# Later DRAM transposing and a later sum beside accumulating loads, in a pooled-attention and MoE kernel

## The chip, the cores and the metric

One core of one Trainium2 chip. The metric is the device time of one execution in microseconds (us); lower is better. Before: 985.83 us, the median of 3 runs (984.55 to 986.24).

## The reference

Four batches of attention, whose keys and values are 4x4 mean-pooled `kv` times a small weight, followed by an MLP with a quick gelu on all 49152 tokens.

```python
kv_pool = kv.reshape(B, H // r, r, W // r, r, C).mean(axis=(2, 4))       # B=4, r=4, C=128
kv_flat = kv_pool.reshape(B, -1, C) @ w_sr
k = v = kv_flat                                                          # 768 keys per batch
a = softmax(1 / sqrt(C) * (q @ k.transpose(0, 2, 1)))                    # 12288 queries per batch
x = (a @ v).reshape(B * S, D)
h = x @ w_in                                                             # d_ff = 2048
out = (h * (1.0 / (1.0 + np.exp(-1.702 * h)))) @ w_out
```

## The kernel before

The program has two rounds: attention on two batches (48 groups of 512 tokens), then the MLP ("MoE") on the same 48 groups. `x`, the attention's result, stays in SBUF, the on-chip memory. TensorE fills three banks of PSUM (the memory that its results go to), ScalarE applies exp or gelu to 128x1536 values at a time, and TensorE multiplies the result by the next weight. The MoE needs `x` transposed. The first 72 of a round's 192 blocks of 128 tokens are transposed on TensorE (`turn`); the other 120 go out to DRAM (the buffer `x_bf`) and come back through the transposing DMA, in six parts of 20 blocks. Both DMAs, and the output stores, are issued by SyncE, in program order:

```python
def put_away(n, m):
    o = LATER + m * PART                                   # LATER, PART = 72, 20
    lo = n * XS * SG + o * T
    nc.sync.dma_start(out=x_bf[lo:lo + PART * T, :].rearrange("(k p) c -> p k c", p=T),
                      in_=x[:, o * T:(o + PART) * T].rearrange("p (k c) -> p k c", k=PART))

def bring_back(n, m):
    ...
    nc.sync.dma_start_transpose(out=x[:, o * T:(o + PART) * T].unsqueeze(1), in_=x_bf[lo:lo + PART * T, :])
```

In the first round's MoE the keys of batches 2 and 3 are made for the second round. Eight steps of two loads each add up `kv` in the DMA (two halves, `i2`; each load but the first of a half accumulates, and waits for the one before it). A `gate`, a tiny memset on VectorE that GpSimd waits for, keeps them one step to a group. Then VectorE adds the two halves, and TensorE transposes the sum:

```python
def add_kv(b, n):
    i, w = divmod(n, r)
    ...
    for i2 in range(2):
        nc.gpsimd.dma_start(out=kv_sums[b][:, i2], in_=kv_p[b, i, w, :, i2],
                            **({"accum_op": ADD} if n else {}))

def sum_kv(b, a):
    t = kv_sums[b][:, :, 4 * a:4 * a + 4, :]
    pooled[b, a] = kvtmp.tile([Hp, 4, C], BF, name="pooled")
    nc.vector.tensor_tensor(pooled[b, a], t[:, 0], t[:, 1], ADD)

def use_kv(b, a):
    sum_kv(b, a)
    extras.extend([(transpose_pooled, b, a), (make_k, b, a), (make_v, b, a)])   # TensorE, placed soon after

def background_moe(g):                                     # called as group g's first matmuls are placed
    n, g = divmod(g, 4 * XS)                               # n: round; 4 * XS = 48
    m, odd = divmod(g - 3, 2)
    if 0 <= m < (4 * XS * G // T - LATER) // PART:         # six parts
        (bring_back if odd else put_away)(n, m)
    g += n * 4 * XS
    for b, lo in ((2, 2), (3, 20)):
        if lo <= g < lo + 8:
            gate()
            add_kv(b, g - lo)
        if g in (lo + 9, lo + 13):
            use_kv(b, (g - lo - 9) // 4)
```

A finished group's output is transposed by VectorE into one of three `o_sb` buffers and stored by SyncE in four DMAs. Cuts are marked with dots.

The softmax here doesn't subtract the row's maximum and nothing guards it: scores larger than these inputs give would overflow.

Of the kernel before, what the change touches and what calls it, by code (L numbers as in the profile page):

```python
# [20 lines left out]
def kernel(  # L21
# [134 lines left out]
    def add_kv(b, n):  # L156
        i, w = divmod(n, r)
        if n == 0:
            kv_sums[b] = kvsum.tile([Hp, 2, Wp, C], F32, name="kvs")
# [8 lines that stand above are left out]
# [209 lines left out]
    def gate():  # L377

        nc.vector.memset(gate_tile, 0.0)  # L379
        nc.gpsimd.memset(gate_tile, 0.0)  # L380
# [27 lines left out]
    def background_moe(g):  # L408

        n, g = divmod(g, 4 * XS)  # L410
        m, odd = divmod(g - 3, 2)
        if 0 <= m < (4 * XS * G // T - LATER) // PART:
            (bring_back if odd else put_away)(n, m)
        g += n * 4 * XS
        for b, lo in ((2, 2), (3, 20)):
            if lo <= g < lo + 8:
                gate()
                add_kv(b, g - lo)
            if g in (lo + 9, lo + 13):
                use_kv(b, (g - lo - 9) // 4)  # L420

    def use_kv(b, a):
        sum_kv(b, a)
        extras.extend([(transpose_pooled, b, a), (make_k, b, a), (make_v, b, a)])
# [36 lines left out]
    for n in range(R):  # L461
        part = chunks[n * NA // R:(n + 1) * NA // R]
        while part:
            m = sizes.pop(0) if sizes else K
# [17 lines left out]
    def prepare(p):  # L482

        nonlocal now
        for f, *args in first.get(p, ()):
            if f in COST:
                now = max(now, free[next_acc()])
            f(*args)
            if f in COST:
                now += COST[f][0]  # L490
                free[last_acc] = now + COST[f][1]
        kind, part = seq[p]
        for i, _ in part:
            if (kind, i) not in begun:
                begun.add((kind, i))
                (background if kind == "a" else background_moe)(i)
# [119 lines left out]
```

## Time and profile before

| | kernel before |
|---|---|
| median of 3 runs, us | 985.83 |
| profiled execution: time, span, us | 987.93, 986.1 |
| ScalarE busy, us | 956.0 |
| ScalarE idle before gelu (line L435), us | 8.5 |
| ScalarE idle before exp (L321), us | 11.7 |

In the page's groups the number after the bar is busy time, then the mean of one instruction in ns, then the engine's idle time just before these instructions and what ended it. ScalarE is the bound where its idle time is nearly nil. Times in timelines are microseconds from the span's start. The rows are shown in the prediction below.

### The profile page before, as it was taken

Reading aid. Unit: us, or ns where it says so; the run is one execution under the profiler, and the core shown is the slowest. Engines: PE = TensorE matmul, PEld = TensorE weight load, DVE = VectorE, ACT = ScalarE, POOL = GpSimd, SP = SyncE. Lnnn points to the kernel's source line nnn. Section 1 sums busy time; section 2 is a strip of 40 time slices with the busy share of each in tenths; the row PEclk is TensorE's granted clock in tenths of the full one; section 3 lists DMA queues with packets and bytes.
Section 4 is the critical chain, followed back from the end, with each engine's and each line's share of the span. In section 5 each row is a group of like instructions: output and inputs, shape, how many; then the busy total and the mean of one; then the engine's idle time right before and its main releaser. Section 6 shows DMA issues by size and latency. Waiting matters only on the chain.

```text
span 986.1 us, 15763 instructions
## 1 busy us (share of the span) xinstructions
PE 963.7 (98%) x6431; PEld 513.1 (52%) x6431; DVE 207.7 (21%) x506; ACT 956.0 (97%) x713; POOL 65.4 (7%) x113
## 2 busy tenths in 40 slices
PE   7899999997999999999999999999999999999997
PEld 3567777543444444444447777754444444444443
DVE  4444333201110111101114433320111010101010
ACT  4999999996999999999999999999999999999997
POOL 3100101320002310000000000000000000000000
PEclk9999999998999999999999999999999999999999
DMA  9897764999628972222276432025772222222222
GB/s 181 160 200 147 108 118 85 121 164 178 115 35 121 157 97 43 35 41 43 41 105 113 86 77 59 2 38 110 136 141 40 44 43 33 38 39 34 41 32 43
DMA packets 335688, 84.99 MB, mean 86 GB/s; under 512 B 309568, under 2 KB 333248, under 8 KB 335296
## 3 DMA queue, kind: packets, MB, share of 16 engines
q1 hardware_dynamic: 305456, 51.34, 31.1%
q0 software_dynamic: 29104, 32.51, 22.0%
q8 instruction: 50, 0.82, 0.3%
q10 hardware_dynamic: 1056, 0.13, 0.1%
q14 instruction: 22, 0.18, 0.1%
HBM read 52.49 MB, written 43.52 MB: 97 GB/s over the span
## 4 chain that ended last, share of the span: by engine, by line
PE 62%; ACT 26%; DMA 5%; issue 4%; DVE 1%; POOL 1%; POOLq 0%; DVEq 0%; ACTq 0%
ACT ag L435 24%; PE banks L440 19%; PE banks L433 18%; PE banks L330 12%; PE banks L319 12%; DMA kvs<-in_kv_dram 4%; ACT ag L321 2%; POOL kvs L161 1%; PE banks L356 1%; DMA x<-in_q_dram 1%; DVE qT L224 1%; PE banks L218 0%; PE banks L129 0%; PE banks L265 0%; DVE xt L346 0%
## 5 line engine op out<-in xcount | busy, mean ns | idle before, releaser
L435 ACT ACTIVATE ag<-banks 128x1536 bf16<-128x1536 f32 x512 | 690.1, 1531 | 8.5 <-PE banks L433 8.5
L433 PE MATMUL banks<-x,w_in_sb 128*128 128x512 bf16 x1536 | 415.9, 379 | 0.4 <-ACT ag L435 0.3
L440 PE MATMUL banks<-ag,w_out_sb 128*128 128x512 bf16 x1536 | 411.5, 380 | 0.5 <-ACT ag L435 0.5
L321 ACT ACTIVATE ag<-banks 128x1536 bf16<-128x1536 f32 (+2 forms) x196 | 260.2, 1451 | 11.7 <-PE banks L319 11.3
L440 PEld LDWEIGHTS <-w_out_sb 128*128 128x128 bf16 x1536 | 149.9, 98 | 180.6 <-issue 1.4
L433 PEld LDWEIGHTS <-w_in_sb 128*128 128x128 bf16 x1536 | 148.4, 98 | 180.4 <-issue 24.1
L447 DVE STREAM_TRANSPOSE o_sb<-banks 128x512 f32<-128x512 f32 x96 | 68.8, 716 | 554.2 <-PE banks L440 554.2
L330 PEld LDWEIGHTS <-ag 128*128 128x128 bf16 x2304 | 150.2, 97 | 48.1 <-issue 1.5
L330 PE MATMUL banks<-v,ag 128*128 128x129 bf16 x2304 | 168.7, 220 | 0.7 <-DVE v L153 0.7
L319 PE MATMUL banks<-qT,kT 128*128 128x512 bf16 x576 | 155.8, 378 | 5.7 <-ACT ag L321 4.1
L319 PEld LDWEIGHTS <-kT 128*128 128x128 bf16 x576 | 48.9, 97 | 33.5 <-issue 4.2
L338 DVE RECIPROCAL rec<-banks 128x3 f32<-128x3 f32 x128 | 23.0, 180 | 132.3 <-PE banks L330 132.3
L346 DVE TENSOR_TENSOR x<-banks,rec 128x384 bf16<-128x384 f32 x80 | 44.6, 558 | 2.8
L161 POOL DMA_DIRECT2D kvs<-in_kv_dram x32 | 40.2, 1307 | 36.9 <-DMA kvs<-in_kv_dram 34.0
L380 POOL MEMSET gate_tile<- 1x8 f32 x38 | 4.5, 119 | 458.0 <-DVE gate_tile L379 458.0
L346 DVE TENSOR_TENSOR xt<-banks,rec 128x384 bf16<-128x384 f32 x48 | 26.8, 558 | 1.7
L358 DVE COPY x<-banks 128x768 bf16<-128x768 bf16 x24 | 13.4, 558 | 24.5 <-PE banks L356 24.5
L356 PE MATMUL banks<-ident,xt 128*128 128x128 bf16 x144 | 11.9, 218 | 0.0
L224 DVE COPY qT<-banks 128x512 bf16<-128x512 bf16 x15 | 9.8, 687 | 5.0 <-PE banks L218 4.9
L195 POOL DMA_DIRECT2D q_bf<-in_q_dram x20 | 9.9, 496 | 5.3 <-DMA x<-in_q_dram 1.9
L356 PEld LDWEIGHTS <-xt 128*128 128x128 bf16 x144 | 9.3, 97 | 1.4
L218 PE MATMUL banks<-ident,x 128*128 128x128 bf16 x64 | 6.0, 224 | 2.6 <-DVE qT L224 1.9
(56 smaller groups left out, 87.7 us busy)
## 6 DMA issues: line engine op xcount, KB each, us to landing
out_dram<-o_sb SPq DMA_DIRECT2D x382, 64.0 KB, 2.0
kvs<-in_kv_dram POOLq DMA_DIRECT2D x32, 384.0 KB, 6.4
q_bf<-in_q_dram POOLq DMA_DIRECT2D x20, 512.0 KB, 6.5
x_bf<-x SPq DMA_DIRECT2D x12, 640.0 KB, 4.7
x<-in_kv_dram POOLq DMA_DIRECT2D x12, 512.0 KB, 12.4
x<-in_q_dram POOLq DMA_DIRECT2D x3, 512.0 KB, 20.3
w_in_sb<-in_moe_w_in_dram POOLq DMA_DIRECT2D x1, 512.0 KB, 5.1
w_out_sb<-in_moe_w_out_dram POOLq DMA_DIRECT2D x1, 512.0 KB, 7.6
```

The costliest lines, as they stand in the source:

```text
L161: nc.gpsimd.dma_start(out=kv_sums[b][:, i2], in_=kv_p[b, i, w, :, i2], **({"accum_op": ADD} if n else {}))
L224: nc.vector.tensor_copy(dst, src)
L319: nc.tensor.matmul(ps[:, k, :], kTs[i // GB][:, jc * 128:(jc + 1) * 128], rhs, start=True, stop=True)
L321: nc.scalar.activation(place([("a",) + c for c in chunks]), ps, AF.Exp, scale=scale)
L330: nc.tensor.matmul(av_of[u][:, k * (C + 1):(k + 1) * (C + 1)], weights(("a", i, jc))[:, o:o + T], vs[i // GB][:, jc, 0:C + 1], start=(jc = ...
L338: nc.vector.reciprocal(rec, ps[:, :, C])
L346: nc.vector.tensor_tensor(to, ps[:, :, 0:C], rec.unsqueeze(2).broadcast_to([128, TS, C]), MUL)
L356: nc.tensor.transpose(ps[:, k, :], xt[:, k, :], ident)
L433: nc.tensor.matmul(ps[:, k, :], w_in_sb[:, fc * 128:(fc + 1) * 128], x[:, g % (4 * XS) * G:(g % (4 * XS) + 1) * G], start=True, stop=True)
L435: nc.scalar.activation(place([("m",) + c for c in chunks]), ps, AF.Gelu_apprx_sigmoid)
L440: nc.tensor.matmul(o_of[g], w_out_sb[:, fc, :], weights(("m", g, fc)), start=(fc == 0), stop=(fc == FCH - 1))
L447: nc.vector.transpose(o_sb, o_of.pop(g))
```

## The change

Its intent: keep the DRAM transposing away from the accumulating loads. Batch 2's loads run at groups 2 to 9, so the transposing begins at group 9; batch 3's loads begin at group 24, after the last part has come back at group 20. The two sums of each batch also move: for batch 2 from groups 11 and 15 to 12 and 14, for batch 3 from 29 and 33 to 34 and 36. No instruction is added or removed (15763 in both).

```diff
-        m, odd = divmod(g - 3, 2)
+        m, odd = divmod(g - 9, 2)
...
-        for b, lo in ((2, 2), (3, 20)):
+        for b, lo in ((2, 2), (3, 24)):
...
-            if g in (lo + 9, lo + 13):
-                use_kv(b, (g - lo - 9) // 4)
+            if g in (lo + 10, lo + 12):
+                use_kv(b, (g - lo - 10) // 2)
```

## The prediction

> **What bounds the kernel now.** I read the page first, part 1 and then part 5. The program is two rounds of attention (two batches each) and mixture-of-experts (MoE, 48 groups each); ScalarE applies exp and gelu to 128x1536 blocks of PSUM.
>
> ```profile
> PE 963.7 (98%) x6431; PEld 513.1 (52%) x6431; DVE 207.7 (21%) x506; ACT 956.0 (97%) x713; POOL 65.4 (7%) x113
> ...
> L435 ACT ACTIVATE ag<-banks 128x1536 bf16<-128x1536 f32 x512 | 690.1, 1531 | 8.5 <-PE banks L433 8.5
> ...
> L321 ACT ACTIVATE ag<-banks 128x1536 bf16<-128x1536 f32 (+2 forms) x196 | 260.2, 1451 | 11.7 <-PE banks L319 11.3
> ```
>
> PE and ACT are both nearly full, but the PE figure is padded: matmuls of 128x512 start 0.22 us apart and are recorded as 0.38 us long. ACT is the bound: 956.0 of 986.1 us, and its idle time in the MoE is only 8.5 us. The 11.7 us of the exp line lie before and in the first groups, which the change does not touch. So only those 8.5 us can be won here. Whose are they? Next the waits, restricted to 218 to 250 us, and ACT's timeline there (start, length, engine, line, count, idle before in brackets):
>
> ```profile
> ACT ag L435 <- PE banks L433: 8.5, 2, 7.5
> PEld L172 <- DVE pooled L167: 6.9, 1, 6.9
> PE banks L172 <- DVE pooled L167: 6.4, 1, 6.4
> ```
>
> ```profile
> 149.12 79.55 ACT L435 ACTIVATE ag<-banks 128x1536 bf16<-128x1536 f32 x59
> 236.15 1.45 ACT L435 ACTIVATE ag<-banks 128x1536 bf16<-128x1536 f32 x1 [7.48 <-PE banks L433]
> 238.60 41.87 ACT L435 ACTIVATE ag<-banks 128x1536 bf16<-128x1536 f32 x31 [1.00 <-PE banks L433]
> ```
>
> It is one stall. PE's timeline has its last matmul before it at 226.21 and then the transposes of `pooled` at 233.42; DVE's timeline shows why:
>
> ```profile
> 222.31 0.72 DVE L447 STREAM_TRANSPOSE o_sb<-banks 128x512 f32<-128x512 f32 x1 [5.97 <-PE banks L440]
> 232.67 0.69 DVE L167 TENSOR_TENSOR pooled<-kvs 96x512 bf16<-96x512 f32 x1 [9.64 <-DMA kvs<-in_kv_dram]
> ```
>
> Group 11's program step puts the sum of the two halves of batch 2's `kvs` on DVE; it was reached at 223.0 and waited until 232.7 for the last accumulating load. PE executes in order, so its transposes held up the next matmuls, and ACT ran dry. The chain of waits passes through the same loads (DMA kvs 4.5% of the span).
>
> Why are the loads late? GpSimd's timeline, the last four issues:
>
> ```profile
> 208.68 1.31 POOL L161 DMA_DIRECT2D kvs<-in_kv_dram  x1 [8.20 <-DMA kvs<-in_kv_dram]
> ...
> 217.22 1.31 POOL L161 DMA_DIRECT2D kvs<-in_kv_dram  x1 [4.63 <-DMA kvs<-in_kv_dram]
> ...
> 225.21 1.31 POOL L161 DMA_DIRECT2D kvs<-in_kv_dram  x1 [3.49 <-DMA kvs<-in_kv_dram]
> ```
>
> The chain of waits gives the landing time behind each: 14.62 us for the load issued at 193.68, then 8.26, 7.70 and 7.37. SyncE's timeline shows transfers through `x_bf` in the same microseconds: a DMA transpose at 192.96, a store to `x_bf` at 204.66, a transpose at 216.31. For batch 3, which runs beside output stores alone, the 16 loads land in a median of 6.3 us and at most 8.0; batch 2's median is 7.4, its longest 14.6.
>
> **What the Trainium skill says.** "DMA: Bandwidth & Descriptors", section "Queues, rings and completion order": each DMA engine round-robins, packet by packet, between the queue rows with work. Loads (software queue) and `x_bf` traffic plus stores (SyncE's hardware queue) therefore share 16 engines; the trace agrees, by the 14.6 against 8.0 us. Same page, "Anatomy of one DMA": DMA engines wait on no semaphore, the issuing sequencer does so before dispatch. GpSimd's 8.20 us ahead of the issue at 208.68 agree: each accumulating load waits there for the one before it into the same half, so a delay is passed to the rest. "TensorE: Matmul & The Clock Gate", "What's actually happening": after an idle window of about 3.4 us PE is throttled to half rate. Here PE idled 6.39 us, the granted clock of 236 to 239.5 us is 0.65, and three matmuls cover 1.49 us where they otherwise cover 0.81. That explains ACT's second gap, 1.00 us.
>
> **The change, part by part.** One group's output transposes on DVE are mostly 6.69 us apart, and a whole group costs ACT 16/3 x 1.343 us = 7.16 us (690.1/512 = 1.348 per activation as a check). A step placed at group g on DVE or SyncE follows the output of group g-6 (the sum of group 11 follows the sixth output at 222.31).
>
> 1. Transposing moves from groups 3 to 14 to groups 9 to 20. Nothing is added: the same 12 stores and 12 transposes, the same loads, no instruction more or less. The first store goes behind group 3's output (DVE ends it at 209.65), so at about 211.7 us, after four store issues of some 0.5 us.
> 2. Batch 2's loads keep groups 2 to 9. Alone with the stores they should behave like batch 3's: there the last gate opens at 347.92, the last issue is 351.13, and with 6.3 us to landing it ends at 357.4, 9.5 us after the gate. Batch 2's last gate opens at 209.5, so the loads should be down by 219. The first `x_bf` store meets just the last pair; at 8.5 us for these instead of 6.3, and one waiting for the other, I put the landing at 219 to 225.
> 3. The first sum moves from group 11 to 12: it then follows the seventh output, 222.31 + 6.69 = 229.0, so about 229.7. The margin is 5 to 10 us, and PE wants the result about 3 us later still (223.0 to 226.2 + 0.8 in the old run). So the stall is gone: 7.48 + 1.00 = **8.5 us less**, one for one at the end, as ACT is the bound from there on.
> 4. The second sum moves from group 15 to 14, two groups (some 14 us) after the first. The three extras of one sum took 233.4 to 238.7 after the stall and 265.3 to 268.6 the second time, under 9 us from their sum to the last copy. No collision: 0.
> 5. Batch 3's loads move from groups 20-27 to 24-31, clear of transposing that now ends at about group 20. Last landing: 357.4 - 8.5 + 4 x 7.16 = 377.5; its sum at group 34: 361.1 - 8.5 + 5 x 7.16 = 388.4. Margin 11 us against 3.7 now. Attention on batch 2 starts at 504.3, batch 3 some 65 us later. Worth 0.
> 6. Round 2 has the same move with no loads beside it, so 0.
>
> Sum: 985.83 - 8.5 = 977.3 us, 0.86% faster.
>
> **The rivals.** (a) The wait moves instead of going: the first `x_bf` store and transpose stretch the last pair of loads. Speaking for it: one load took 14.6 us in the neighbourhood of a transpose. Against: it would have to land after 229.7 to hold DVE and after 233 to hold PE, 23 us after its gate; only one pair, not four, meets the traffic. If so, 1 to 4 us of the stall stay: 978.5 to 981.5.
> (b) Transposing now comes too late for the MoE groups that read it. The first part holds blocks 72 to 91, which group 18 reads first. ACT starts group 18 at about 149.1 + 18 x 7.16 = 278 us; the transpose is issued at about 219 to 222, ends by 232. Later parts follow at two groups each and are wanted at five groups each, so the margin grows from 45 us. If it failed, tens of microseconds would be lost, over 2%; I see nothing for it.
> (c) SyncE as the new bound: a transpose occupies its issue for 2.2 to 6.4 us, and a transpose must wait there for its `x_bf` store, ahead of output stores; with three output buffers DVE would wait, then PSUM, then PE. In the run before, group 3's output left SyncE at 221.64, 12 us after it was ready, and no wait came of it. After 236 us, with transposing but without loads, the stores left about 2 us late (group 7's output starts on DVE at 245.85, its stores at 247.82). So 0, at worst 1 to 2 us.
> (d) The stall was never the loads' fault but the step's: a sum at group 11 is simply early. Then moving the sum alone gains most of it: in the old traffic it would wait from 229.7 to 232.6, and PE hardly at all. This speaks for the same total; it divides the credit between two parts of the diff.
>
> **Range and chances.** The three times before lie between 984.55 and 986.24. The centre is 977.3. Downwards there is only noise, as there is no other ACT idle time in reach: 975.9. Upwards rival (a) or a little of (c): 980.0. Reaching 2% faster (966) would need 20 us, more than ACT's idle time in all the MoE; 2% slower would need rival (b). Chances 0.01, 0.98, 0.01.
>
> **What would show it.** In the page, ACT L435's idle time falls from 8.5 to under 1 us while its busy time stays at 690; the waits of `pooled` for DMA and of PE for `pooled` vanish; the longest landing of batch 2's loads is below 10 us; SyncE's first `x_bf` store stands near 212 instead of 139 us; DVE's first sum near 229.7, second near 243. It would be wrong if L435 shows a new idle time ended by L433 around 230 or 278 us, or if DVE's output transposes wait for a DMA. If the time falls by less than 7 us with the idle time gone, activations became longer, and my reading of ACT as bound is what failed.

## More of the kernel before

The profiled execution of the kernel before took 987.93 us, of which the profile's span covers 986.1.

## The result, and the profile after

The changed kernel: 980.08 us, the median of 4 runs (979.09 to 980.60), beside 985.19 us for the kernel before over its four runs. The ratio is 0.9949 with a 95% interval of 0.9931 to 0.9967. (A ratio is the mean time of one kernel's fast runs over that of the other's of the same rounds, so not quite the ratio of the medians.) That is 5.1 us less, not 8.5, and 0.08 us outside the range.

The trace, though, shows the stall gone, as the prediction said. The same two groups of ScalarE on the page of the changed kernel:

```profile
L435 ACT ACTIVATE ag<-banks 128x1536 bf16<-128x1536 f32 x512 | 689.9, 1538 | 0.3 <-PE banks L433 0.2
...
L321 ACT ACTIVATE ag<-banks 128x1536 bf16<-128x1536 f32 (+2 forms) x196 | 260.3, 1455 | 11.3 <-PE banks L319 10.8
```

Gelu's idle time fell from 8.5 to 0.3 us at the same busy time. VectorE's timeline of the changed kernel at the place of the old stall:

```profile
221.79 0.72 DVE L447 STREAM_TRANSPOSE o_sb<-banks 128x512 f32<-128x512 f32 x1 [5.97 <-PE banks L440]
228.49 0.72 DVE L447 STREAM_TRANSPOSE o_sb<-banks 128x512 f32<-128x512 f32 x1 [5.97 <-PE banks L440]
229.13 0.65 DVE L167 TENSOR_TENSOR pooled<-kvs 96x512 bf16<-96x512 f32 x1
```

The sum now stands behind the seventh output instead of the sixth and has no bracket, that is, no idle time before it: the loads had landed. GpSimd's last issues for batch 2 (two loads in one row) and SyncE's first store to `x_bf`, from the timelines of the two engines:

```profile
212.51 2.73 POOL L161 DMA_DIRECT2D kvs<-in_kv_dram  x2 [3.20 <-DMA kvs<-in_kv_dram]
```

```profile
212.35 1.17 SPq L366 DMA_DIRECT2D x_bf<-x  x1
```

The last load is issued at 213.9 us, where the kernel before issued it at 225.21. It met that one `x_bf` store (and, at the very end, the first transpose, issued at 223.64) and took some 12 us (the median of the last two in the DMA view of 211 to 216 us), so it landed near 226, 3 us ahead of the sum.

The profiled spans differ by 986.1 - 977.3 = 8.8 us: 8.2 of gelu idle time, 0.4 of exp idle time, 0.2 of the rest. So the open question is why the runs differ by 5.1 us and the profiles by 8.8. The profiled execution of the kernel before (987.93 us) was slower than each of its four other runs (983.50 to 986.24); that of the changed kernel (979.09) was the fastest of its four. Of the 3.7 us between the two differences, 2.7 are thus the first kernel's (987.93 - 985.19) and 1.0 the second's (980.08 - 979.09).

### The profile page after: what moved, and what is told of

Its sections match the earlier page's. It is cut to its first block, busy times and chain, and to the rows that moved or that the text cites. A ratio compares the mean times of both kernels' runs of the same rounds, so it can differ in the third digit from the quotient of the medians.

```text
span 977.3 us, 15763 instructions
## 1 busy us (share of the span) xinstructions
PE 960.9 (98%) x6431; PEld 511.9 (52%) x6431; DVE 207.7 (21%) x506; ACT 955.9 (98%) x713; POOL 65.5 (7%) x113
## 4 chain that ended last, share of the span: by engine, by line
PE 76%; ACT 21%; issue 1%; DVE 1%; DMA 1%; POOL 0%; POOLq 0%
PE banks L433 24%; PE banks L440 24%; ACT ag L435 19%; PE banks L330 14%; PE banks L319 12%; ACT ag L321 1%; PE banks L356 1%; DVE qT L224 1%; DMA x<-in_kv_dram 1%; PE banks L129 0%; PE banks L218 0%; PE banks L265 0%; DVE pooled L167 0%; DVE xt L346 0%; PE banks L172 0%
## 5 line engine op out<-in xcount | busy, mean ns | idle before, releaser
L435 ACT ACTIVATE ag<-banks 128x1536 bf16<-128x1536 f32 x512 | 689.9, 1538 | 0.3 <-PE banks L433 0.2
L321 ACT ACTIVATE ag<-banks 128x1536 bf16<-128x1536 f32 (+2 forms) x196 | 260.3, 1455 | 11.3 <-PE banks L319 10.8
```

What stands on the lines that cost most here:

```text
L321: nc.scalar.activation(place([("a",) + c for c in chunks]), ps, AF.Exp, scale=scale)
L435: nc.scalar.activation(place([("m",) + c for c in chunks]), ps, AF.Gelu_apprx_sigmoid)
```

## The experiments

Two theories. **A:** the stall is the landing of the last load less the moment TensorE wants the sum; that landing differs from run to run, and the profile that I read had caught a longer stall than the timed runs beside it. The changed kernel has none in any run. **B:** the stall is 8.5 us in every run, and the changed kernel gives back some 3.5 us elsewhere in the executions that were not profiled. The parts of the diff are also run one by one. All eight kernels gave correct results.

### before_again: the kernel before, unchanged

> The kernel before, unchanged, for a second profile and more times. Theory A (the stall differs from run to run, and the profile that was read caught a long one): ScalarE's idle time on the gelu line is not 8.5 us again but 3 to 7, and the profiled run's time less that idle time is 978.5 to 981. Theory B (the stall is 8.5 us in every run, and the changed kernel gives back some 3.5 us elsewhere): idle 8 to 9 us again, time less idle time near 977. Both: ratio 1.000 within 0.002.

Measured: 985.67 us median of 6 runs (981.41 to 991.86); the kernel before, over 11 more runs beside this and the next three kernels, 987.47 (982.17 to 991.18); ratio 0.9996 (0.9961 to 1.0031). The profiled execution took 985.10 us. Its waits between 218 and 250 us, each with total, number of times and longest:

```profile
...
DVE pooled L167 <- DMA kvs<-in_kv_dram: 7.0, 1, 7.0
ACT ag L435 <- PE banks L433: 6.0, 3, 4.8
PEld L172 <- DVE pooled L167: 4.2, 1, 4.2
PE banks L172 <- DVE pooled L167: 3.7, 1, 3.7
```

The same chain as before, load to sum to transposes to gelu, and 2.5 us shorter: 6.0 us instead of 8.5. Theory B expected 8 to 9 here. 985.10 - 6.0 = 979.1, within A's range. The runs of this one kernel spread over 10.5 us.

### traffic_only: the transposing alone moves

```diff
-        m, odd = divmod(g - 3, 2)
+        m, odd = divmod(g - 9, 2)
```

> Only the DRAM transposing moves (first store at group 9 instead of 3); sums stay at groups 11 and 15, batch 3 at group 20. If the transposing traffic is what makes the loads late, the stall shrinks to 0 to 2 us although the sum stays early: the last pair of loads should land at 225 to 227 as in the changed kernel, DVE's sum waits from about 222.5 to there, PE is wanted at about 226. Time within 0.2% of the changed kernel (979.5 to 982). If the step of the sum is the cause, the stall stays at 5 to 8.5 us and the time at 985.

Measured: 979.12 us median of 6 (978.46 to 980.43), ratio 0.9923 (0.9897 to 0.9950); the median is 0.4 us under the expected range. Gelu's idle time is 0.0 (the last number of the first line). In VectorE's timeline the early sum is still there, behind the sixth output:

```profile
L435 ACT ACTIVATE ag<-banks 128x1536 bf16<-128x1536 f32 x512 | 689.8, 1533 | 0.0
```

```profile
221.72 0.72 DVE L447 STREAM_TRANSPOSE o_sb<-banks 128x512 f32<-128x512 f32 x1 [5.97 <-DMA out_dram<-o_sb]
223.41 0.69 DVE L167 TENSOR_TENSOR pooled<-kvs 96x512 bf16<-96x512 f32 x1 [0.98 <-DMA kvs<-in_kv_dram]
```

It waits 0.98 us instead of 9.64, and ScalarE, whose idle time is 0.0, notices nothing. So the traffic through `x_bf` is what made the loads late, and moving it is enough by itself. The wait for an output store on the first row of the timeline costs no time, as the output was not ready sooner (the spacing to the row before is 6.69 us as ever).

### sum_only: the sums of batch 2 alone move

```diff
-        for b, lo in ((2, 2), (3, 20)):
+        for b, lo, sums in ((2, 2, (12, 14)), (3, 20, (29, 33))):
...
-            if g in (lo + 9, lo + 13):
-                use_kv(b, (g - lo - 9) // 4)
+            if g in sums:
+                use_kv(b, sums.index(g))
```

> Only batch 2's sums move (groups 12 and 14 instead of 11 and 15); the transposing stays at group 3, batch 3 at group 20. Loads land as late as before (about 230 to 233), the sum is reached at about 229.7 and waits up to 3 us, PE wants it at about 233. So the stall is 0 to 2 us and the time 979.5 to 982, if a step of 6.7 us is enough. If the traffic has to move, the time stays above 983. Should the output stores, late on SyncE beside the loads, be a bound of their own (rival c), DVE's seventh output transpose shows a wait for a DMA.

Measured: 979.43 us median of 6 (978.52 to 981.51), ratio 0.9925 (0.9896 to 0.9954). Its profiled execution was the slowest of the six. VectorE's timeline:

```profile
223.48 0.72 DVE L447 STREAM_TRANSPOSE o_sb<-banks 128x512 f32<-128x512 f32 x1 [5.97 <-PE banks L440]
232.09 0.72 DVE L447 STREAM_TRANSPOSE o_sb<-banks 128x512 f32<-128x512 f32 x1 [7.90 <-DMA out_dram<-o_sb]
234.11 0.69 DVE L167 TENSOR_TENSOR pooled<-kvs 96x512 bf16<-96x512 f32 x1 [1.29 <-DMA kvs<-in_kv_dram]
```

This is the prediction's rival (c), alive: the third row shows the sum waiting 1.29 us for its load, but the second shows an output transpose held for 7.90 us by an `o_sb` buffer whose store SyncE had issued late. It is 8.61 us behind the output before, instead of 6.69, so some 2 us late, and a further such wait (1.29 us, for the next output) reached TensorE and left gelu 1.2 us idle. The kernel before shows no such wait; its seventh output came only at 239.21, after the stall, so one of this length could not have shown. The loads are no earlier than before (last issue at 228.02): one group's delay of the sum is simply as long as the stall.

### batch3_only: batch 3 alone moves

```diff
-        for b, lo in ((2, 2), (3, 20)):
+        for b, lo, sums in ((2, 2, (11, 15)), (3, 24, (34, 36))):
...
```

> Only batch 3's loads move (groups 24 to 31, sums at 34 and 36). Both theories: nothing, ratio 0.998 to 1.002, as batch 3 stalls nothing in either trace. It is also one more profile of batch 2's stall, under theory A anywhere from 3 to 9 us, with time less idle time at 978.5 to 981; under theory B 8.5 us, and near 977.

Measured: 988.74 us median of 6 (982.36 to 991.85), ratio 1.0009 (0.9975 to 1.0044): worth nothing, as expected. The profile has 8.2 us of gelu idle time. Time less idle, 989.24 - 8.2 = 981.0, sits at the upper edge of A's range, because exp idled 13.3 us in this execution, where six of the ten profiles have 11.1 to 11.7.

### after_again: the changed kernel, more runs

> The changed kernel once more, on one chip with the kernel before, so that their ratio rests on many runs. Theory A (the kernel before has a stall that differs from run to run, 6.0, 8.2 and 8.5 us in three profiles; the changed one has none): 978.5 to 981.0 in all runs, ScalarE's gelu line idle under 1 us, the kernel before 983 to 991 with a wider spread, ratio 0.991 to 0.996. Span less the idle times of the gelu and exp lines: 965.8 within 0.3, as in all six profiles so far. Theory B (something given back elsewhere in unprofiled runs): a profile with a wait that the first did not show.

Measured, on another chip than the four runs above, where the kernel before has 11 runs with a median of 986.92 us (983.02 to 991.13): 978.96 us median of 6 (978.77 to 979.40), ratio 0.9920 (0.9893 to 0.9946). Gelu idles 0.3 us again. So here the gain is 8.0 us, and the changed kernel spreads over 0.6 us where the other spreads over 8.1. Theory B finds nothing: the profile shows no wait that the first did not.

### sum_at_10: the first sum of batch 2 one group earlier

The edit is that of sum_only with (10, 15) for batch 2.

> Batch 2's first sum one group earlier than before (10 instead of 11), all else as before. If the stall is the landing of the last load less the moment PE wants the sum, it grows by one output spacing, 6.7 us: gelu line idle 12 to 17 us, time 989 to 998, ratio to before 1.005 to 1.008. If the time does not follow the idle time one for one, ScalarE is not the bound from there on.

Measured: 995.69 us median of 4 (993.90 to 995.70), ratio 1.0084 (1.0053 to 1.0114), a hair above the expected range. ScalarE's timeline at the stall:

```profile
209.20 13.63 ACT L435 ACTIVATE ag<-banks 128x1536 bf16<-128x1536 f32 x10
237.08 1.45 ACT L435 ACTIVATE ag<-banks 128x1536 bf16<-128x1536 f32 x1 [14.25 <-PE banks L433]
239.53 6.91 ACT L435 ACTIVATE ag<-banks 128x1536 bf16<-128x1536 f32 x5 [1.00 <-PE banks L433]
```

14.25 + 1.00 us, 6.8 more than the 8.5 of the first profile, for a sum that stands one output, 6.7 us, earlier (by medians it is 8.8 us, over a kernel whose own stall varies). The loads' last issue (227.62) did not move to earlier. This is the formula of theory A with its other term changed.

### traffic_at_6: transposing half as far

```diff
-        m, odd = divmod(g - 3, 2)
+        m, odd = divmod(g - 6, 2)
```

> Transposing begins at group 6 (three groups later than before, three earlier than changed), sums and batch 3 as before. In the old trace the parts at groups 3 and 4 ran in the attention stage, at 139 to 156 us, and cost the loads nothing; what meets the loads is the traffic at groups 6 to 10 (190 to 226 us). Beginning at 6 puts as many stores and transposes into those groups. So no gain: gelu line idle 4 to 11 us, ratio 0.996 to 1.004. If instead the stall shrinks with every group of delay, it should be about half: idle 2 to 5 us, ratio 0.994 to 0.997.

Measured: 987.78 us median of 4 (986.04 to 988.66), ratio 1.0006 (0.9975 to 1.0037); gelu idle 8.5 us. Half the move gains nothing. SyncE's timeline says why:

```profile
191.85 0.79 SPq L366 DMA_DIRECT2D x_bf<-x  x1
...
204.56 3.44 SPq L372 DMA_TRANSPOSE x<-x_bf  x1
...
213.26 2.05 SPq L366 DMA_DIRECT2D x_bf<-x  x1
...
224.39 4.38 SPq L372 DMA_TRANSPOSE x<-x_bf  x1
```

The stretch from 190 to 226 us, in which batch 2's later loads run, holds two stores and two transposes; the kernel before had two transposes and two stores in it as well (192.96, 204.66, 216.31, 225.70), because its first two stores and first transpose ran at 139 to 150 us, in the hand-over from attention to MoE. In these two kernels, then, the stall follows not when the transposing begins but how much of it falls among the loads.

### sum_at_13: the first sum two groups later, old traffic

The edit is that of sum_only with (13, 15) for batch 2.

> Old traffic, batch 2's first sum two groups later than before (13), the second stays at 15. The sum is reached at about 236, after the last landing at 229 to 235, so no wait for a load. If the waits of DVE's output transposes for output stores, which the run with the sum at 12 showed (7.9 and 1.3 us), are a bound of their own, they are here too, and ScalarE idles 0.5 to 2 us. Otherwise 0 to 0.3. Time 978.5 to 981.5 in both cases, ratio 0.990 to 0.995.

Measured: 979.89 us median of 4 (978.39 to 980.29), ratio 0.9925 (0.9895 to 0.9956). The sum waits for no load. VectorE waits twice for output stores, 12.5 us in total and 6.8 at most, and gelu's idle time is 0.0: here these waits cost nothing. Of the two expected outcomes the second one came. So such waits need not cost anything; in sum_only's one profile they cost 1.2 us. Why there and not here was not followed up.

### All ten profiles together

| kernel | time | span | gelu idle | exp idle | span less both |
|---|---|---|---|---|---|
| before | 987.93 | 986.1 | 8.5 | 11.7 | 965.9 |
| before_again | 985.10 | 983.3 | 6.0 | 11.5 | 965.8 |
| batch3_only | 989.24 | 987.5 | 8.2 | 13.3 | 966.0 |
| traffic_at_6 | 987.61 | 985.8 | 8.5 | 11.2 | 966.1 |
| sum_at_10 | 995.69 | 993.9 | 15.3 | 12.8 | 965.8 |
| changed | 979.09 | 977.3 | 0.3 | 11.3 | 965.7 |
| after_again | 979.00 | 977.2 | 0.3 | 11.1 | 965.8 |
| traffic_only | 978.54 | 976.8 | 0.0 | 11.1 | 965.7 |
| sum_only | 981.51 | 979.7 | 1.2 | 12.8 | 965.7 |
| sum_at_13 | 979.97 | 978.2 | 0.0 | 12.5 | 965.7 |

The last column is constant within 0.4 us while the spans differ by 17. This is bookkeeping (ScalarE's span is its busy time plus its idle time), but it says that no activation became longer and that no third idle time matters, so in these ten executions theory B has no room. Against it in the others speak the 6.0 us of before_again and the six times of after_again, all within 0.4 us of its profiled one. In the seven profiles with the transposing begun at group 3 or 6 the last load lands (its issue plus its time to landing in the trace) at 229.5 to 234.8 us, in the three with it begun at group 9 at 223.3 to 226.4: that is what moving the traffic does. No version beats the changed kernel clearly: traffic_only has the same idle time within 0.3 us, and what is left, the exp line's 11 to 13 us, is at the start of the program.

## Why the prediction was right or wrong

**Right: the cause, and what each part does.** The one stall, its chain and its end are as told. The first `x_bf` store came at 212.35 us (told: 211.7), the first sum at 229.13 (229.7), the second at 244.06 (243), both sums without a wait. Batch 3's last loads, issued at 368.09, took 6.9 us in the median and its sum began at 391.96 (told: 388.4), and batch3_only gained nothing; round 2 was not tried alone, but had no gelu idle time to win. Rivals (a) and (b) did not come: the time of 980.08 lies in (a)'s 978.5 to 981.5, but its mechanism, a stall that stays, is not in the trace.

**Wrong: step 3's "8.5 us less", and the sum "985.83 - 8.5 = 977.3" that rests on it.** The 8.5 us were the stall of one execution, the profiled one; the 985.83 us were the median of three others. That profiled execution had itself taken 987.93 us. Taken from its own time, the stall gives 987.93 - 8.5 = 979.4 us, and the changed kernel's medians are 980.08 and 978.96. The mis-sized term is the stall: 8.5 us in one profile, 6.0 in another, 8.2 in a third whose batch 2 is untouched; and from times, 981.41 to 991.86 over the six runs of the unchanged kernel against a floor near 979, it lies between about 2 and 13 us (an estimate, as these runs' traces were not kept, and the exp line's idle time is in it). In the four timed runs of the first comparison (983.50 to 986.24) it was, against the same floor, some 4.5 to 7 us. The gain is accordingly 5.1 us there, and 8.0 in the second comparison, with eleven runs of the kernel before.

Which of the two was unusual? Neither by much. Over the 28 later runs of the unchanged kernel on two chips the median is 986.88 us; ten are slower than the profiled 987.93, and eight are faster than the first comparison's median of 985.19. So the stall in the profile was not an exceptional one; the few timed runs happened to be short (or ran on a chip where it is shorter). The forecast of 977.3 lies 1.7 us from the second comparison's 978.96 and 2.8 from the first's 980.08: that one lies inside the range and the other just outside is the luck of the draw, and the error in the working is the same.

**A sign of being wrong that came.** The prediction said that if the time fell by less than 7 us with the idle time gone, activations had become longer and the reading of ScalarE as the bound had failed. The time fell by 5.1 us with the idle time gone, but gelu's busy time is 689.9 us beside 690.1 and exp's 260.3 beside 260.2. The reading of the bound held; the sign had left out a stall that varies. (The 1.343 us per activation in the prediction stands in no view; 690.1/512 is 1.348, and no step hangs on the difference.)

**Too narrow: the range.** I allowed "only noise" downwards, and upwards only something new. The exp line's idle time, which I set aside as untouched, differs from 11.1 to 13.3 us between executions, and the time follows it. In the first comparison the changed kernel's four spans were 977.3, 977.8, 978.8 and 978.8 us. A slow start of 12 to 13 us would make the latter two; no trace of those was kept, so that is argued, not shown, and a difference between chips is not excluded.

**Two sizes within the steps.** The last pair of loads was to take 8.5 us each beside the first `x_bf` store and took about 12 (12.5 at most, where the prediction named under 10 as its sign), so the margin at the sum was 3 us and not 5 to 10; in after_again's profile the last load took 10.0 and the margin was about 5. And rival (c), put at 0, is not always 0: 1.2 us in sum_only's profile, none in the changed kernel's two.

**Not split in advance, but told as rival (d):** each of two edits removes the whole stall alone (979.12 and 979.43 us), so their gains do not add. Together they left room in these profiles: the sum came 3 us after the landing, where with either edit alone it still waited, 0.98 and 1.29 us. Whether the `x_bf` stores, the transposes or the output stores bunched up behind them hurt the loads most was not tried and stays open.

## What to carry to other kernels

The stall here, which ended with a DMA among other DMAs, was a draw and not a constant. So take such a stall from the time of the very execution whose profile shows it, or profile the same kernel two or three times, before subtracting it from a median. A late producer can be cured on either side, as here, by clearing the transfers that share its time or by placing the consumer one step later; try the two apart. When traffic is moved out of the way, count how much of it is left within the critical loads' stretch: moving its start by three groups left as many transfers there (four) and gained nothing.

## What the Trainium skill lacked or had wrong

- "DMA: Bandwidth & Descriptors", section "Anatomy of one DMA": its fit for the software path, 2.0 us plus bytes over 436 thousand per us, gives an estimate of 2.9 us for one load of 384 KB. The page gives the fit per DMA; the loads here run in pairs, and all but the first pair of a batch accumulate. Over the ten traces no accumulating load landed in less than 5.5 us; in the kernel before, a batch's 16 loads took a median of 6.3 us beside output stores, and beside `x_bf` traffic 7.4, with 14.6 the longest. The page gives no figure for accumulating loads, nor for loads beside a transposing DMA.
- Same page, section "Issuing engines are not separate DMA queues": the time in which a sequencer issues a DMA "is usually small relative to the DMA itself". Here a transpose from `x_bf` held SyncE for 2.1 to 9.9 us while its landing took some 5 to 15 us, and the output stores behind it started late enough to hold VectorE for 7.9 us in one profile.
- No page says how much such a contended wait differs between executions of one kernel on one chip: here 983.02 to 991.13 us over eleven runs, against 978.77 to 979.40 over six of the changed kernel, without the wait.
